# Loading the fifth granule's keys and queries ahead of the fourth granule's values

## The chip, the cores and the metric

The kernel runs on one core of a Trainium2 chip. The core has a matrix engine (TensorE, PE in the profile; its weight loads are PEld), a vector engine (VectorE, DVE), a scalar engine (ScalarE, ACT), GpSimd (POOL) and SyncE (SP), each with its own instruction stream in program order, and 16 DMA engines that serve several queues. The metric is the time of one execution on the device in microseconds (us); less is better. Four runs of the kernel before gave 208.94, 208.99, 209.06 and 209.45 us, median 209.03.

## The reference

Local attention with a few global keys, followed by a two-layer network. There are 4 batches, 8 heads, 768 positions and heads of 64 (q, k and v in float32).

```python
scores = (q @ k.T) / sqrt(64) - slope[h] * dist
keep   = (col < 8) | (0 <= row - col < 96)      # 8 global keys, a window of 96
a      = softmax(where(keep, scores, -1e9))
x      = (a @ v)                                # 4, 8, 768, 64 -> 3072 x 512
h      = relu(x @ w_in)                         # 512 x 2048
out    = (s * h * h + b) @ w_out                # 2048 x 512, float32
```

## The kernel before

The 3072 rows are cut into 12 granules of 256 positions (two blocks of 128), numbered j = 0 to 11, three per batch; granule j = 3 is the fourth, the first of batch 1, and j = 4 the fifth. A granule has 4 units, one per pair of heads, numbered u = 4j to 4j + 3. For a unit, `stage_S` multiplies keys and queries into a tile `ps_s`, ACT takes the exponential into `pt`, DVE multiplies a mask, and `stage_A` multiplies `pt` by the values into `ps_av` (L494) and normalizes the result into `xn`. `scores(s)` does `stage_S` for units 2s and 2s + 1. Scores need keys and queries with the head dimension on the partitions (`kx`, `qx`), while the loads bring them with the positions there (`nat`); so they are transposed: granules 0 to 3 by PE (`qk_first`, `qk_block`, `qk_wide`), granules from 4 on by four DMA transposes each on SP's queue (`qk_by_dma`, L359). Values are used as loaded, from `vbuf` (tile `vb`), one buffer per batch and two in turn. For a granule that isn't the first of its batch, `make_koff` (L382) and `make_voff` (L395) copy shifted keys and values; granule 4 thus also reads the values of granule 3.

The attention output is transposed (`xT`), and the network follows: `p1` (L618) is the first product with relu and square, `p2` (L666) the second; from granule 4 on the second product is done for pairs of granules by a scheme of seven half products (L818).

All loads of keys, queries, values and weights convert float32 to bfloat16 and stand in POOL's queue, in program order. A granule is six loads of 128 KB (as stored): `load_granule` (L110, its key and query loads at L116, the values through `load_v`, L104, at L108) issues keys and queries of block 0, keys and queries of block 1, then the two value loads. `load_qk` (L99) issues keys and queries of one block alone (L102). The weights and granules 0 to 3 are issued before any computation (L196 to L220), granules 4 and 5 from L1076 on, and granules 6 to 11 by `finish_granule` (L949), each after a gate that waits for earlier work. Nothing on POOL lies between the loads of granule 3 and those of granule 4, so the four granules 2 to 5 are one sequence of 24 loads on that engine.

The order on the other engines is written by hand (`manual_schedule`). Around the change: `qk_wide(3, ...)` at L1110 and L1113 transposes granule 3; SP takes `qk_by_dma(4)` (L1106), `load_scalars` (L1107) and `qk_by_dma(5)` (L1126) in this order; PE does `scores(6)` and `scores(7)` (granule 3), `stage_A(12)` to `stage_A(15)` (granule 3's values), `x_by_pe(3)`, and then `scores(8)` (L1135), the first that reads granule 4's transposes. `scores(10)`, in `step(9)`, is the first that reads granule 5's.

Of the kernel before, what the change touches and what calls it, by code (L numbers as in the profile page):

```python
# [17 lines left out]
def kernel(  # L18
# [21 lines left out]
    GB = 2  # L40
# [41 lines left out]
    def nat_tile(j):  # L82
        if j not in nat:
            nat[j] = ldp.tile([P, 2, GB, H, D], BF16, name="nat", tag=f"nat{j % 4}", bufs=1)
        return nat[j]
# [3 lines left out]
    def rows_of(src, b, sb):  # L89
        return src[b, :, sb * P : (sb + 1) * P, :].rearrange("h p d -> p h d")  # L90
# [8 lines left out]
    def load_qk(j, i):  # L99
        b, g = divmod(j, NGR)  # L100
        for n in range(2):
            nc.gpsimd.dma_start(nat_tile(j)[:, n, i, :, :], rows_of(srcs[n], b, g * GB + i))  # L102

    def load_v(j, blocks=range(GB)):  # L104
        b, g = divmod(j, NGR)
        for i in blocks:
            sb = g * GB + i
            nc.gpsimd.dma_start(vbuf[b % 2][:, sb, :, 0:D], rows_of(v, b, sb))  # L108

    def load_granule(j):  # L110
        b, g = divmod(j, NGR)
        t = nat_tile(j)
        for i in range(GB):
            sb = g * GB + i
            for n in range(2):
                nc.gpsimd.dma_start(t[:, n, i, :, :], rows_of(srcs[n], b, sb))  # L116
        load_v(j)
# [99 lines left out]
    for i in range(4):  # L217
        load_w_out(i, 4)
    load_granule(2)
    load_granule(3)  # L220

# [712 lines left out]
    def run(cs):  # L936
        for c in cs:
            c()
# [134 lines left out]
    run(sums[5:6])  # L1073
    p1[1][7]()
    run(sums[6:7])
    load_granule(4)  # L1076
    load_granule(5)
    template(range(H))
    lo = FC - FC // 4
# [167 lines left out]
```

The softmax here doesn't subtract the row's maximum and nothing guards it: scores larger than these inputs give would overflow.

## Time and profile before

| what | us |
|---|---|
| median of four runs | 209.03 |
| the profiled execution | 209.45 |
| its span, first to last instruction | 207.7 |
| PE busy | 202.0 |
| DVE busy | 160.3 |
| ACT busy | 128.7 |
| POOL busy | 69.9 |

The span is shorter than the time by 1.75 us, which lie ahead of the first and behind the last instruction. Lines of the profile name an instruction by engine, line of the kernel (L440), operation, and the tiles it writes and reads (`out<-in`); POOL's lines for loads are the time in which it writes out the transfer, not the transfer itself, whose time from issue to landing is asked for separately. SPq is SP's queue. `[0.64 <-DMA qx<-nat]` means that the engine was idle for 0.64 us and that a transfer ended the wait. In rows by stretches of time the columns are the length, the busy time of PE, PEld, DVE, ACT and POOL with the number of instructions, the granted clock, the share of the DMA engines and GB/s.

### The profile page before, as it was taken

The page shows a single profiled execution, that of the slowest core. Times are in us where ns is not written, and L with a number is a line of the kernel's source. Part 1 is how long each engine was busy: PE and PEld are TensorE (multiplying, and loading weights), DVE is VectorE, ACT ScalarE, POOL GpSimd, SP SyncE. Part 2 cuts the span into 40 slices and gives each one's busy share as a digit, 9 for nine tenths or more (in the row PEclk, how much of TensorE's full clock was granted, in tenths as well). Part 3 has the DMA queues.
Part 4 walks back from the last instruction along what each step waited for, and adds up shares of the span by engine and source line. Part 5 has one row for each costly group of instructions (what it writes and reads, how often), then busy time and mean ns, then how long its engine had stood idle before and what let it go on. Part 6 is the DMA issues. An engine that isn't in the chain of part 4 may idle for free.

```text
span 207.7 us, 5323 instructions
## 1 busy us (share of the span) xinstructions
PE 202.0 (97%) x2191; PEld 160.2 (77%) x2191; DVE 160.3 (77%) x336; ACT 128.7 (62%) x200; POOL 69.9 (34%) x90
## 2 busy tenths in 40 slices
PE   7899999999989999999999999999999999999993
PEld 2678884557866685778888898888898889888883
DVE  7686589977979955799799974699865696737974
ACT  4975669486975648786564495664695764476200
POOL 8986334899644300904700906300000000000000
PEclk9999999999999999999999999999999999999999
DMA  5999999999999999999999999995460300240006
GB/s 164 172 179 201 206 208 176 156 154 131 118 150 120 154 156 210 124 234 225 126 208 157 112 149 245 161 191 63 52 205 0 92 17 0 52 153 0 0 7 198
DMA packets 110836, 28.17 MB, mean 136 GB/s; under 512 B 97852, under 2 KB 109308, under 8 KB 110812
## 3 DMA queue, kind: packets, MB, share of 16 engines
q0 software_dynamic: 76000, 13.11, 88.2%
q1 hardware_dynamic: 33612, 14.13, 37.9%
q10 hardware_dynamic: 1200, 0.59, 1.1%
q8 instruction: 17, 0.28, 0.6%
q14 instruction: 7, 0.06, 0.1%
HBM read 27.26 MB, written 6.29 MB: 162 GB/s over the span
## 4 chain that ended last, share of the span: by engine, by line
PE 69%; DMA 20%; POOL 6%; SPq 2%; issue 1%; DVE 0%; POOLq 0%
PE ps L618 30%; PE ps L818 24%; DMA w_out_bf<-in_moe_w_out_dram 8%; PE ps L666 7%; DMA qx<-nat 4%; PE ps_s L440 4%; DMA vb<-in_v_dram 4%; PE ps_av L494 4%; DMA nat<-in_k_dram 3%; SPq L359 2%; POOL vb L108 2%; POOL nat L102 2%; POOL nat L116 1%; POOL w_in_bf L140 1%; PE ps_last L818 0%
## 5 line engine op out<-in xcount | busy, mean ns | idle before, releaser
L618 PE MATMUL ps<-xT,w_in_bf 128*128 128x256 bf16 x768 | 90.4, 273 | 0.0
L628 ACT ACTIVATE gT<-ps 128x512 bf16<-128x512 f32 x96 | 55.7, 598 | 46.8 <-PE ps L618 46.6
L618 PEld LDWEIGHTS <-w_in_bf 128*128 128x128 bf16 x768 | 73.0, 98 | 9.5 <-DVE xT L593 0.2
L449 ACT ACTIVATE pt<-ps_s 128x1024 bf16<-128x1024 f32 (+1 forms) x44 | 39.3, 945 | 3.4 <-PE ps_s L440 3.4
L666 PE MATMUL ps<-w_out_bf,gT 128*128 128x512 bf16 x128 | 29.7, 380 | 0.0
L456 DVE TENSOR_TENSOR pt<-pt,tmpl 128x1024 bf16<-128x1024 bf16 (+1 forms) x40 | 24.6, 646 | 4.5 <-ACT pt L449 4.3
L818 PEld LDWEIGHTS <-gsum 128*128 128x128 bf16 x256 | 24.2, 98 | 3.7 <-DVE gsum L781 0.5
L108 POOL DMA_DIRECT2D vb<-in_v_dram x24 | 21.4, 906 | 7.6 <-DMA w_out_bf<-in_moe_w_out_dram 3.3
L792 DVE TENSOR_TENSOR gT<-gT 128x1024 bf16<-128x1024 bf16 x20 | 13.7, 687 | 11.7 <-ACT gT L628 11.7
L666 PEld LDWEIGHTS <-gT 128*128 128x128 bf16 x128 | 11.8, 98 | 13.0
L465 DVE TENSOR_TENSOR xn<-ps_av,rc 128x256 bf16<-128x256 f32 x48 | 20.4, 425 | 1.7
L818 PEld LDWEIGHTS <-gT 128*128 128x128 bf16 x200 | 18.6, 98 | 2.3
L116 POOL DMA_DIRECT2D nat<-in_q_dram x20 | 18.0, 900 | 6.8 <-DMA nat<-in_q_dram 3.0
L116 POOL DMA_DIRECT2D nat<-in_k_dram x20 | 17.8, 890 | 6.4 <-DMA w_in_bf<-in_moe_w_in_dram 2.5
L464 DVE RECIPROCAL rc<-ps_av 128x4 f32<-128x4 f32 x48 | 8.6, 179 | 12.2 <-PE ps_av L494 10.3
L494 PEld LDWEIGHTS <-pt 128*128 128x128 bf16 x320 | 14.4, 97 | 2.7 <-DVE xn L465 0.7
L631 DVE TENSOR_TENSOR gT<-gT 128x512 bf16<-128x512 bf16 x32 | 13.0, 422 | 3.7 <-ACT gT L628 3.3
L494 PE MATMUL ps_av<-vb,pt 128*128 128x65 bf16 x208 | 15.4, 193 | 0.0
L818 PE MATMUL ps<-w_out_bf,gsum 128*128 128x256 bf16 x128 | 15.3, 273 | 0.0
L818 PE MATMUL ps<-wsub,gsum 128*128 128x256 bf16 x128 | 15.1, 273 | 0.0
L122 POOL COPY gate<-xT 1x1 bf16<-1x1 bf16 x6 | 1.9, 320 | 38.6 <-DMA xT<-xn 37.6
L818 PE MATMUL ps<-w_out_bf,gT 128*128 128x256 bf16 x120 | 13.9, 273 | 0.0
(111 smaller groups left out, 220.6 us busy)
## 6 DMA issues: line engine op xcount, KB each, us to landing
out_dram<-o_q SPq DMA_DIRECT2D x15, 256.0 KB, 2.4
vb<-in_v_dram POOLq DMA_DIRECT2D x24, 128.0 KB, 7.4
nat<-in_k_dram POOLq DMA_DIRECT2D x22, 128.0 KB, 6.5
nat<-in_q_dram POOLq DMA_DIRECT2D x22, 128.0 KB, 6.9
w_out_bf<-in_moe_w_out_dram POOLq DMA_DIRECT2D x4, 512.0 KB, 16.2
w_in_bf<-in_moe_w_in_dram POOLq DMA_DIRECT2D x4, 256.0 KB, 7.6
w_in_bf<-in_moe_w_in_dram POOLq DMA_DIRECT2D x2, 512.0 KB, 11.3
out_dram<-o_sb SPq DMA_DIRECT2D x4, 256.0 KB, 6.1
```

Source lines behind the costliest of these rows:

```text
L108: nc.gpsimd.dma_start(vbuf[b % 2][:, sb, :, 0:D], rows_of(v, b, sb))
L116: nc.gpsimd.dma_start(t[:, n, i, :, :], rows_of(srcs[n], b, sb))
L449: nc.scalar.activation(pt[:, :, 0:ncol], ps[:, :, 0:ncol], ACT.Exp, scale=QSCALE)
L456: nc.vector.tensor_tensor(pv, pv, m.rearrange("p h a c -> p h (a c)"), ALU.mult)
L465: nc.vector.tensor_tensor(dst, av[:, :, :, 0:D], rc[:].to_broadcast((P, 2, 2, D)), ALU.mult)
L494: nc.tensor.matmul(av[:, i, hi, 0 : D + 1], lhsT=pt[:, hi, c * P : (c + 1) * P], rhs=vv, start=(n == 0), stop=(n == len(terms) - 1),)
L618: nc.tensor.matmul(ps[:, i, :], lhsT=w_in_bf[:, kc, fc * P : (fc + 1) * P], rhs=xT[j][:, kc, :], start=(kc == 0), stop=(kc == KC - 1),)
L628: nc.scalar.activation(gs, ps[:], ACT.Relu)
L631: nc.vector.tensor_tensor(gs, gs, gs, ALU.mult)
L666: nc.tensor.matmul(po[:], lhsT=g_of(j)[:, fc, tb * P : (tb + 1) * P], rhs=w_out_bf[:, fc, :], start=(fc == 0), stop=(fc == FC - 1),)
L792: outs.append(lambda: nc.vector.tensor_tensor(gs, gs, gs, ALU.mult))
L818: nc.tensor.matmul(ps[:, tb, cs], lhsT=stat[:, fc, tb * P : (tb + 1) * P], rhs=mov[:, fc, cs], start=(fc == 0), stop=(fc == NH - 1),)
```

## The change

The two value loads of granule 3 are taken out of the opening loads and put behind the key and query loads of granule 4. The sequence on POOL was: k, q, k, q of granule 3, v, v of granule 3, k, q, k, q of granule 4, v, v of granule 4, granule 5. It becomes: k, q, k, q of granule 3, k, q, k, q of granule 4, v, v of granule 3, v, v of granule 4, granule 5.

```diff
@@ -217,7 +217,8 @@
     for i in range(4):
         load_w_out(i, 4)
     load_granule(2)
-    load_granule(3)
+    for i in range(GB):
+        load_qk(3, i)
@@ -1073,7 +1074,10 @@
     run(sums[5:6])
     p1[1][7]()
     run(sums[6:7])
-    load_granule(4)
+    for i in range(GB):
+        load_qk(4, i)
+    load_v(3)
+    load_v(4)
     load_granule(5)
     template(range(H))
```

## The prediction

> **What bounds the kernel now.** I read the page's totals first, then the chain, then the PE timeline at the place where the chain leaves PE, then POOL's and SP's timelines with the time each transfer took to land.
>
> ```profile
> PE 202.0 (97%) x2191; PEld 160.2 (77%) x2191; DVE 160.3 (77%) x336; ACT 128.7 (62%) x200; POOL 69.9 (34%) x90
> ...
> PE 69%; DMA 20%; POOL 6%; SPq 2%; issue 1%; DVE 0%; POOLq 0%
> ```
>
> PE is busy for 97% of the span at a granted clock of 0.999, so a change of load order can give back only gaps. Yet 20% of the chain is DMA. The chain's answer shows where:
>
> ```profile
> 40.28 6.70 DMA nat<-in_k_dram
> 46.99 0.02 issue
> 47.00 1.30 SPq L359
> ...
> 49.66 1.70 SPq L359
> ...
> 51.40 8.78 DMA qx<-nat
> 60.18 0.04 issue
> 60.22 0.57 PE ps_s L440 x14
> ```
>
> From 60.22 us to the end the chain is PE without a break worth counting. Before that it is: POOL's first key load of granule 4 (the fifth), issued at 40.28 and landed at 47.0; four transposes on SP (qk_by_dma(4)); the last one, issued at 51.40, lands at 60.18; scores(8) starts on it. That is the only place after the opening where a load stops PE. The PE timeline there, and the same group of instructions for the next scores, where nothing stopped it:
>
> ```profile
> 59.35 0.23 PE L440 MATMUL ps_s<-qx,kx 64*128 64x128 bf16 x2
> 60.22 0.34 PE L440 MATMUL ps_s<-qx,kx 64*128 64x128 bf16 x6 [0.64 <-DMA qx<-nat]
> 60.39 0.40 PE L440 MATMUL ps_s<-qx,ko 64*128 64x128 bf16 x8
> 60.72 0.39 PE L666 MATMUL ps<-w_out_bf,gT 128*128 128x512 bf16 x1
> ...
> 69.35 0.40 PE L440 MATMUL ps_s<-qx,kx 64*128 64x128 bf16 x8
> 69.58 0.39 PE L440 MATMUL ps_s<-qx,ko 64*128 64x128 bf16 x8
> 69.90 0.39 PE L666 MATMUL ps<-w_out_bf,gT 128*128 128x512 bf16 x1
> ```
>
> From the first score matmul to the next product it is 60.72 - 59.35 = 1.37 us with the wait and 69.90 - 69.35 = 0.55 us without. The stall costs 0.82 us, more than the 0.64 printed, because a modelled matmul end covers part of it. PE wants the transposed queries at about 59.4 and gets them at 60.18.
>
> **The change, part by part.** Nothing is added or taken away: the same loads, transposes and stores. Eight of POOL's loads change places, and only among themselves, since POOL has nothing else between granule 3's queries and granule 5. Their slots:
>
> ```profile
> 37.84 0.88 POOL L108 DMA_DIRECT2D vb<-in_v_dram  x1
> 39.17 0.87 POOL L108 DMA_DIRECT2D vb<-in_v_dram  x1 [0.45 <-DMA nat<-in_q_dram]
> 40.28 0.87 POOL L116 DMA_DIRECT2D nat<-in_k_dram  x1 [0.24 <-issue]
> 41.34 1.01 POOL L116 DMA_DIRECT2D nat<-in_q_dram  x1 [0.19 <-issue]
> 42.35 0.88 POOL L116 DMA_DIRECT2D nat<-in_k_dram  x1
> 43.21 0.90 POOL L116 DMA_DIRECT2D nat<-in_q_dram  x1
> ```
>
> The last two slots, for granule 4's values, follow at 44.08 and 44.97. Asking the trace slot by slot for the time to landing (7.3, 6.9, 6.7, 6.5, 6.4, 6.4, 6.4 and 6.2 us), the eight land at 45.1, 46.1, 47.0, 47.8, 48.75, 49.6, 50.5 and 51.2. All move 128 KB, all cost POOL 0.87 to 1.01 us, and POOL's waits here are on loads already under way, so a slot keeps its time whichever load stands in it. POOL's sum: 0.
>
> *Moved up:* granule 4's keys and queries take slots 1 to 4 instead of 3 to 6. The four landings go from 47.0, 47.8, 48.75, 49.6 to 45.1, 46.1, 47.0, 47.8: 1.7 to 1.9 us earlier.
>
> *Moved back:* granule 3's values take slots 5 and 6, landing at 48.75 and 49.6 instead of 45.1 and 46.1. Their first reader is stage_A(12), on PE at 53.16: 3.5 us to spare before contention. Granule 4's values stay in slots 7 and 8 (first reader make_voff(4), on DVE at 63.29), and granule 5's keys stay at 45.81.
>
> *What follows on SP:* its queue stands 45.2 us on the first key load, so qk_by_dma(4) starts 1.9 us earlier, at 45.1. Behind it are the two scalar loads and qk_by_dma(5). How much of the 1.9 us reaches the end of the transposes is the one term that the trace doesn't price directly. The transposes' packets (queue q1) first appear just before 50.0, 2.9 us after SP issued them, and then comes a bad patch:
>
> ```profile
> 48.00:50.00 2.00, 2.00 (x26) 1.31 (x24) 1.83 (x6) 1.37 (x2) 2.00 (x3) 1.00 2.68 151
> 50.00:52.00 2.00, 2.00 (x27) 1.64 (x27) 0.96 (x3) 2.00 (x5) 2.00 (x4) 1.00 1.82 106
> 52.00:54.00 2.00, 2.00 (x37) 1.78 (x34) 1.86 (x5) 2.00 (x5) 1.81 (x3) 1.00 4.20 55
> 54.00:56.00 2.00, 2.00 (x24) 1.75 (x19) 1.86 (x7) 1.99 (x4) 0.88 (x1) 1.00 2.01 162
> ```
>
> The last column is GB/s: 151, 106, 55, 162. A 16 KB transfer of the instruction queue starts at 50.5, and from 51 to 53.7 everything crawls; another starts at 62.2 and 62 to 64 shows the same (97 GB/s). I take that patch as fixed in time. Started at 48.0, q1 has about 450 packets more behind it when the patch begins than the 260 of before (252 in the window 50 to 51 now, about 400 per us later, in 58 to 59). At 400 per us those 450 are 1.1 us; the data of the second transpose would end some 1.4 us earlier. Upper end: all 1.9 us. Lower end: 0, if the patch begins with the transposes rather than with the instruction transfer. I take 1.2 us: the last transpose lands at 60.18 - 1.2 = 59.0, before PE's 59.4. The stall goes whole at any value from 0.8 up.
>
> *What the earlier transposes take from the loads.* With both queues running, 58 to 59 shows 430 load packets and 397 transpose packets, against 2374 load packets alone in 48 to 50, or 1187 per us. A load is 1024 such packets (128 KB at 128 bytes): 0.86 us alone, 2.4 us shared. Sharing would start at 48.0; the first load of granule 3's values is then nearly through, the second finishes about 1.6 us later than its slot, 51.2, which still leaves 2 us before 53.16. Bounds: 49.6 (no loss) and 53.9 (the whole 2.7 us patch falls on it as well), the latter 0.7 us too late. I take 0.
>
> The Trainium skill, "DMA: Bandwidth & Descriptors", section "Queues, rings and completion order", has each DMA engine alternate between the queues that have work, packet by packet. That speaks against the change: an earlier transpose takes half the packets of the values behind it. The 430 to 397 above agrees. By strict halves of 1187 per us the second value load would lose 0.9 us, by the row 1.6; neither reaches 53.16.
>
> *What is late next.* With PE 0.8 us ahead, scores(10) wants granule 5's last transpose at 69.41 - 0.82 = 68.6. It was issued at 59.45 and took 9.6 us: 69.05. If it does not move, PE stalls there for 0.46 us and 0.36 of the gain is left. It queues behind granule 4's transposes (issue at 59.45, 8 us under way), so I expect about 1 us of their lead to reach it: 0. Bounds 0 and +0.46. DVE and ACT are not in the way: make_koff(4) ends at 59.5, ACT's copy at 60.1, and the exponential follows the scores.
>
> *Sum* against the profiled execution: 209.45 (span 207.7 and 1.75 around it) - 0.82 = 208.63. That execution lies 0.42 above the median of the four, 209.03; on the median the sum is 208.21. If part of the 0.42 is a longer stall in the profiled execution, the others have less to win, down to 208.63 again. I take 208.35.
>
> **The rivals.**
> 1. *The stall shrinks or moves on* (18%): the transposes win only 0.3 to 0.7 us, or scores(10) waits up to 0.46. For it: slacks of 0.4 at both places. Against it: one chain of transposes feeds both. Gain 0.2 to 0.5 us: 208.5 to 208.8.
> 2. *Nothing moves* (10%): the crawl follows the transposes' start and sets their end. For it: GB/s falls 1 us after q1 starts. Against it: the same patch at 62 to 64 comes 1.5 to 2 us after the second set starts, with another instruction transfer. About 209.0.
> 3. *Slower: granule 3's values late at stage_A(12)* (16%). Place: PE at 53.16, with all later PE work behind it. It decides once the second value load lands after 53.16 plus the 0.82 us won, about 54.0; landing at 55 would cost 1.0 net, 210.0. For it: four slots back and into the start of the transposes; loads issued at 51 to 59 took 11.5 to 15.4 us to land. Against it: loads issued at 42.35 and 43.21 landed in 6.4.
> 4. Anything else that costs (4%), such as a crawl that now hits granule 5's loads as well: 209.5 to 210. A gain over 0.9 us: 2%.
>
> **How the numbers follow.** My forecast, the stall gone whole, has 50%: 208.1 to 208.65. What a measurement here can tell from no change is 0.2%, 0.42 us: faster is below 208.61, slower above 209.45. Faster: 47 of the forecast's 50, 9 of rival 1's 18, 2 for the larger gain: 58%. Same: 3 + 9 + 10 = 22%. Slower: 16 + 4 = 20%. The range must hold 80%: from 208.1 it takes the forecast, rivals 1 and 2 (78%) and the cheapest part of rival 3, to 209.4.
>
> **What would show it.** Right: POOL's keys and queries of granule 4 at 37.8 to 41.3, SP's first L359 near 45.1, the last transpose of granule 4 landed before 59.4, no wait of PE's L440 on qx, and 0.55 us between scores(8) and the next product. Wrong: a wait of PE's L494 on vb near 53 (rival 3), L440 waiting on qx near 60 (rivals 1 and 2) or near 68.6 (rival 1), or crawling windows that start 1 us after q1 does, wherever that is (rival 2).

## The result, and the profile after

| | median us | runs | span of the profiled execution |
|---|---|---|---|
| before | 209.34 | 56 | 207.7 |
| after | 208.68 | 35 | 206.7 |

The ratio is 0.9974, 95% interval 0.9964 to 0.9983: 0.54 us faster (0.36 to 0.75), out of 209.34; the two medians are 0.66 us apart. The 56 runs of before hold the four of the forecast, whose median of 209.03 was 0.3 us low. A second comparison (12 runs against 27, below) gave 0.9963 (0.9949 to 0.9977). Ratios leave out executions that ran longer at a lower granted clock, chiefly three of the six (at 0.983 and 0.984) of the version below that has granule 3's values late.

In the page of the changed kernel, the busy totals and the chain by engine:

```profile
PE 201.7 (98%) x2191; PEld 160.1 (77%) x2191; DVE 159.6 (77%) x336; ACT 128.6 (62%) x200; POOL 70.7 (34%) x90
...
PE 95%; DMA 2%; DVE 1%; ACT 0%; issue 0%
```

PE has the same 2191 matmuls and nearly the same busy time (201.7 against 202.0 us), in a span 1.0 us shorter. DMA's 20% of the chain has become 2%, all of it in the opening: from 5 us to the end nothing but PE (with a copy or two of DVE and ACT) is on it. PE's timeline at scores(8) and at scores(10) (the changed kernel has four lines more, so L440 is now L441 and L666 is L667):

```profile
59.27 0.40 PE L441 MATMUL ps_s<-qx,kx 64*128 64x128 bf16 x8
59.51 0.39 PE L441 MATMUL ps_s<-qx,ko 64*128 64x128 bf16 x8
59.83 1.90 PE L667 MATMUL ps<-w_out_bf,gT 128*128 128x512 bf16 x8
...
68.45 0.40 PE L441 MATMUL ps_s<-qx,kx 64*128 64x128 bf16 x8
```

From the first score matmul to the next product it is 59.83 - 59.27 = 0.56 us where it was 1.37, and the eight matmuls that stood as two and six are one group. PE starts scores(8) 0.08 us earlier than before and ends it 0.89 earlier; scores(10) is 0.90 earlier, and SP's last stores start 0.91 earlier (203.17 against 204.08). So 0.81 of the 0.91 us is the stall; 0.08 was there ahead of scores(8) and is put down to scatter of the opening. POOL's and SP's timelines show where the lead comes from:

```profile
38.13 0.87 POOL L102 DMA_DIRECT2D nat<-in_k_dram  x1
38.99 0.88 POOL L102 DMA_DIRECT2D nat<-in_q_dram  x1
39.86 1.09 POOL L102 DMA_DIRECT2D nat<-in_k_dram  x1
41.12 1.03 POOL L102 DMA_DIRECT2D nat<-in_q_dram  x1 [0.17 <-issue]
42.14 3.51 POOL L108 DMA_DIRECT2D vb<-in_v_dram  x4
```

```profile
45.00 1.31 SPq L360 DMA_TRANSPOSE kx<-nat  x1
46.36 1.31 SPq L360 DMA_TRANSPOSE qx<-nat  x1
47.71 1.37 SPq L360 DMA_TRANSPOSE kx<-nat  x1
49.12 1.76 SPq L360 DMA_TRANSPOSE qx<-nat  x1
...
59.81 1.22 SPq L360 DMA_TRANSPOSE qx<-nat  x1
```

And the fourth transpose, with the time from its issue to its landing:

```profile
L360 SPq DMA_TRANSPOSE qx<-nat x1: 1757/1757/1757, 49.1 to 49.1; - x1
DMA to landing us min/median/max: 9.2/9.2/9.2
```

SP's first transpose of granule 4 starts at 45.00 instead of 47.00. The last, issued at 49.12, took 9.2 us and landed at 58.3, against 60.18 before and against the 59.33 at which PE wants it. Granule 3's two value loads landed at 48.5 and 49.3, well before 53.1.

### The profile page after: what moved, and what is told of

Same layout as the page of the kernel before. It is cut to its first block, busy times and chain, and to the rows that moved or that the text cites. A ratio compares the mean times of both kernels' runs of the same rounds, so it can differ in the third digit from the quotient of the medians.

```text
span 206.7 us, 5323 instructions
## 1 busy us (share of the span) xinstructions
PE 201.7 (98%) x2191; PEld 160.1 (77%) x2191; DVE 159.6 (77%) x336; ACT 128.6 (62%) x200; POOL 70.7 (34%) x90
## 4 chain that ended last, share of the span: by engine, by line
PE 95%; DMA 2%; DVE 1%; ACT 0%; issue 0%
PE ps L619 41%; PE ps L819 24%; PE ps L667 14%; PE ps_s L441 6%; PE ps_av L495 5%; DMA first<-in_k_dram 2%; PE ps_t L351 1%; PE ps_s L517 1%; PE ps_x L591 1%; PE ps_s L532 1%; PE ps_av L558 1%; PE ps_t L327 1%; DVE nat L260 0%; PE ps_t L341 0%; PE ps_last L819 0%; DVE kx L331 0%
## 5 line engine op out<-in xcount | busy, mean ns | idle before, releaser
L667 PE MATMUL ps<-w_out_bf,gT 128*128 128x512 bf16 x128 | 29.7, 380 | 0.0
L793 DVE TENSOR_TENSOR gT<-gT 128x1024 bf16<-128x1024 bf16 x20 | 13.7, 687 | 11.7 <-ACT gT L629 11.7
L667 PEld LDWEIGHTS <-gT 128*128 128x128 bf16 x128 | 11.8, 98 | 13.0
L116 POOL DMA_DIRECT2D nat<-in_k_dram x16 | 14.2, 890 | 5.7 <-DMA w_in_bf<-in_moe_w_in_dram 2.4
L116 POOL DMA_DIRECT2D nat<-in_q_dram x16 | 14.3, 895 | 4.7 <-DMA nat<-in_q_dram 2.8
```

What stands on the lines that cost most here:

```text
L667: nc.tensor.matmul(po[:], lhsT=g_of(j)[:, fc, tb * P : (tb + 1) * P], rhs=w_out_bf[:, fc, :], start=(fc == 0), stop=(fc == FC - 1),)
L793: outs.append(lambda: nc.vector.tensor_tensor(gs, gs, gs, ALU.mult))
```

## Experiments

The theory: the change removes the stall at scores(8) by starting granule 4's transposes two load slots earlier, and does nothing else. The rivals: the two profiled executions differ by chance; the last load, not the transposes' queue, sets the end; the values moved back cost something; a second wait at scores(10) eats part of the gain; and the crawl of the transfers (a stretch of about a microsecond or more in which all DMA of the core falls far below its usual 150 GB/s or so), not the order of the loads, is what matters. Diffs are against the changed kernel unless it says otherwise.

**Both kernels again.** No edit.

> The kernel before, for a second profile of it. The first showed 0.82 us lost at scores(8). If the measured gain of 0.54 us is less than that because the stall varies from execution to execution, this profile shows another length of it, with the last transpose of granule 4 landing anywhere from 58.8 to 60.5. If the stall is the same 0.8 us in every execution, the changed kernel must lose some 0.3 us elsewhere.

> A third profile of the kernel before, to the same end: the three lengths of the stall at scores(8) should lie around 0.5 us in the mean if the stall is all that the change removes.

> The changed kernel once more. Theory: the gain is the stall at scores(8) and nothing else, so no wait of the scores line on qx near 59 us; the last transpose of granule 4 landed at 58.3 in the first trace of it, 1 us ahead of PE. The ratio to the kernel before should be 0.9974 again, within 0.002. The theory leaves one doubtful place: granule 5's last transpose landed 0.1 us before scores(10) wanted it (68.4 against 68.5), so this execution may show a wait of up to 0.5 us there. Rival, that the 1 us between the two profiled spans was mostly chance: the scores line waits near 59 again, and the ratio lies within 0.001 of 1.

> Another profile of the changed kernel: no wait on qx at scores(8); at scores(10) a wait between 0 and 0.5 us, by where granule 5's last transpose lands (68.4 in the first one).

PE's timeline at scores(8) in the two further profiles of the kernel before, the first and the second:

```profile
59.31 0.23 PE L440 MATMUL ps_s<-qx,kx 64*128 64x128 bf16 x2
60.66 0.34 PE L440 MATMUL ps_s<-qx,kx 64*128 64x128 bf16 x6 [1.11 <-DMA qx<-nat]
...
61.16 1.69 PE L666 MATMUL ps<-w_out_bf,gT 128*128 128x512 bf16 x6
```

```profile
59.56 0.23 PE L440 MATMUL ps_s<-qx,kx 64*128 64x128 bf16 x2
60.65 0.34 PE L440 MATMUL ps_s<-qx,kx 64*128 64x128 bf16 x6 [0.86 <-DMA qx<-nat]
...
61.15 1.69 PE L666 MATMUL ps<-w_out_bf,gT 128*128 128x512 bf16 x6
```

Measured as before (61.16 - 59.31 and 61.15 - 59.56, less 0.55), the stalls are 1.30 and 1.04 us. With the first profile's 0.82 there are three lengths, and the executions took 209.84, 209.83 and 209.45 us: all three are above the median, and the longer stalls go with the longer times. The last transpose landed at 60.64, 60.64 and 60.18. The mean of the three stalls is 1.05 us, not the 0.5 that was expected of it.

The changed kernel's two further profiles have no wait on qx at either place; the last transpose of granule 4 landed at 58.9 and 58.2, and the one of granule 5 0.8 and 1.3 us ahead of scores(10), against 0.1 in the first. Timed again, the ratio to before was 0.9963 (0.9949 to 0.9977), with the runs of before between 208.55 and 209.94 and those of after between 208.39 and 208.83. So the stall is real and varies from execution to execution; three profiles of the changed kernel show none, and its times scatter less. In the first comparison the changed kernel scatters more than here: 10 of its 35 times lie between 209.02 and 209.96; none of these has been profiled, and what delays them is open. That the gain by the ratios (0.54 and 0.77 us) is below the mean of the three profiled stalls fits executions of before with little or no stall, and the fastest one of before, 208.45 us, is as fast as the fastest of after, 208.44; but none of those has been profiled, so this part is argued, not shown.

**Half of the change.**

```diff
-    for i in range(GB):
-        load_qk(4, i)
+    load_qk(4, 0)
     load_v(3)
+    load_qk(4, 1)
     load_v(4)
```

> Half of the change: only block 0 of granule 4's keys and queries goes ahead of granule 3's values; block 1 keeps its two slots (landing about 48.8 and 49.6). Theory A, the transposes' own queue sets the end: once the first of the four starts 1.9 us early, the third has its input (48.8) long before the queue reaches it (about 54), and the last lands near 58.3, as with the whole change: no stall at scores(8), ratio to before 0.9965 to 0.9985. Theory B, the last load sets the end: the fourth transpose is issued at about 50.1 instead of 51.4 and lands 0.6 us or less earlier than before, near 59.6; some 0.2 us of the stall is left, ratio 0.998 to 1.0.

Ratio 0.9965 (0.9952 to 0.9979): all of the gain. SP's timeline of this run:

```profile
45.09 1.29 SPq L360 DMA_TRANSPOSE kx<-nat  x1
46.42 1.31 SPq L360 DMA_TRANSPOSE qx<-nat  x1
48.66 1.73 SPq L360 DMA_TRANSPOSE kx<-nat  x1
50.43 1.26 SPq L360 DMA_TRANSPOSE qx<-nat  x1
```

and for the last of the four:

```profile
DMA to landing us min/median/max: 8.0/8.0/8.0
```

The last transpose is issued 1.3 us later than with the whole change and takes 8.0 us instead of 9.2: it lands at 58.43, no later than the 58.2 to 58.9 there. So theory A holds. The four transposes behave as if they ran one after the other in their queue: as long as the crawls are the same (more on these below), the start of the first decides when the last ends, and the loads of block 1 need not move.

**The values of granule 3 two slots later, and later still.** In the first, the two value loads change places:

```diff
+    load_v(4)
     load_v(3)
-    load_v(4)
     load_granule(5)
```

> The changed kernel with the two pairs of value loads exchanged: granule 4's first, then granule 3's, two slots later than in the change. Those slots landed at 49.8 and 51.6 in the changed kernel's trace, 1.5 us before stage_A(12) wants granule 3's values (53.1). Theory, a value load costs nothing until it lands after 53.1: no wait of L495 on vb, ratio to before 0.9955 to 0.9975, as the changed kernel. Rival, the spare time is eaten in part of the executions by the crawl near 50: a wait of up to 1 us on vb, and a ratio above 0.998.

Ratio 0.9966 (0.9951 to 0.9982), no wait on vb; the two loads landed at 49.8 and 51.6. In the second, they stand behind granule 5's first keys and queries as well:

```diff
-    load_v(3)
     load_v(4)
-    load_granule(5)
+    load_qk(5, 0)
+    load_v(3)
+    load_qk(5, 1)
+    load_v(5)
```

> The prediction's rival 3 made on purpose. Order: keys and queries of granule 4, values of granule 4, keys and queries of block 0 of granule 5, and only then the two value loads of granule 3, then the rest of granule 5. Granule 3's values stand in the slots that landed at 53.1 and 56.2 in the changed kernel, where stage_A(12) wants them at 53.1. If a late value load holds up PE one to one, PE's L495 waits on vb for 2.5 to 3.5 us near 53 and the kernel is 1.5 to 3 us slower than before (ratio 1.007 to 1.015), scores(8) having no stall. If the wait at stage_A(12) is absorbed (PE's work behind it was waiting for something else anyway), the ratio stays under 1.002.

Ratio 1.0128 (1.0083 to 1.0173), 2.7 us slower than before, from three executions only (211.02, 211.57 and 213.40 us). The second value load landed at 56.2, and PE's timeline has:

```profile
53.44 0.22 PE L495 MATMUL ps_av<-vb,pt 128*128 128x65 bf16 x2
56.23 0.46 PE L495 MATMUL ps_av<-vb,pt 128*128 128x65 bf16 x10 [2.56 <-DMA vb<-in_v_dram]
56.62 0.51 PE L441 MATMUL ps_s<-qx,kx 64*128 64x128 bf16 x12
```

where the changed kernel has:

```profile
53.08 0.53 PE L495 MATMUL ps_av<-vb,pt 128*128 128x65 bf16 x12
53.55 0.51 PE L441 MATMUL ps_s<-qx,kx 64*128 64x128 bf16 x12
```

The wait is passed on one to one: from its first matmul to the next scores, stage_A(12) takes 56.62 - 53.44 = 3.18 us instead of 53.55 - 53.08 = 0.47, which is 2.7 us more, and the span is 209.8 us, 2.8 more than in the changed kernel of the same comparison (207.0). So rival 3 of the forecast is a real mechanism. A landing at 51.6 cost nothing and one at 56.2 cost its whole lateness, which fits the 53.1 us at which PE wants the values; the change, at 49.3, stays 3.8 us on the safe side.

**Granule 5 ahead as well.**

```diff
     load_v(3)
+    for i in range(GB):
+        load_qk(5, i)
     load_v(4)
-    load_granule(5)
+    load_v(5)
```

> One step more than the change: granule 5's four key and query loads also go ahead of granule 4's values (order: keys and queries of 4, values of 3, keys and queries of 5, values of 4, values of 5). Theory: in the changed kernel granule 5's last transpose lands only 0.1 us before scores(10) wants it, and in a good part of the executions later, which is why the measured gain (0.54 us) is less than the 0.9 us of the profiled one. Two slots earlier, its loads land 1.7 us or more earlier, the last transpose lands before 67.5, and the time goes 0.1 to 0.4 us below the changed kernel's (ratio to before 0.9955 to 0.997). Rival: the second wait is not there in most executions (the stall of before is just shorter on the average than in its profile); then the ratio equals the changed kernel's, 0.9974 within 0.0005. Price of the step: granule 4's values, wanted at 63 by DVE, land two to four slots later, by about 59: nothing.

Ratio 0.9964 (0.9952 to 0.9976), the same as the changed kernel beside it (0.9963). Granule 5's last transpose landed at 65.95 instead of 68.4, and nothing came of it. The rival holds: no second wait eats the gain.

**The instruction transfers moved, with the load order of before.** Against the kernel before, one kernel with 36 and one with 18 opening matmuls:

```diff
-    warm(9, 4 * P)
+    warm(36, P)
```

```diff
-    warm(9, 4 * P)
+    warm(18, 2 * P)
```

The columns worked through are the same; PE has 54 or 18 more instructions (a weight load and a matmul for each of 27 or 9).

> The kernel before, with the 9 opening matmuls of 512 columns (on zeros, for warming) made 36 of 128 columns: the same columns, but 54 more instructions on PE, so that the 16 KB transfers of the instruction queue, one for every 256 instructions or so, come some 2.5 us earlier: the one at 50.5 at about 48, before granule 4's transposes move (49.9). Theory F, the crawl of 51 to 53.7 comes from the instruction transfer that meets the transposes: it is gone or much shorter, the last transpose lands at 58 to 59 and the stall at scores(8) goes, without any change of the load order; 0.3 to 0.9 us less, if the opening keeps its length. Theory T, the crawl comes 1 us after the transposes start, whatever the instruction queue does: it stays near 51 to 53, and so do the stall and the time. The changed kernel's trace had one crawl of each kind (49 to 50 with no instruction transfer, 54 to 55 after one at 52.9).

> The kernel before with the opening matmuls made 18 of 256 columns: 18 more instructions on PE, a third of the shift of the 36. The instruction transfer should start near 49.3 instead of 50.5, still beside the first transposes (49.9). Theory, the length of the crawl depends on whether a 16 KB transfer runs while transposes run: the crawl stays 2 to 2.75 us long and the stall stays above 0.4 us; ratio to before 0.999 to 1.001. Rival, any earlier transfer helps in proportion: the stall is cut by about a third, ratio 0.999 to 0.9995 with a last transpose at about 59.9; or the 36 helped by their shape rather than by the shift: no stall here either.

Ratios: 0.9982 (0.9967 to 0.9997) with 36 matmuls, 0.9968 (0.9953 to 0.9983) with 18. Neither profile has a wait of PE on qx, the load order being that of before. With 18, the last transpose landed at 59.05; with 36 at 59.23, just as PE came to it (from the first score matmul to the next product 59.79 - 59.13 = 0.66 us, 0.1 more than without a wait), so that some of the other executions may well have kept a short stall. Rows by 1 us of the kernel before and of the one with 18 matmuls; the last column is GB/s:

```profile
50.00:51.00 1.00, 1.00 (x18) 0.74 (x18) 0.41 (x2) 1.00 (x3) 1.00 (x2) 1.00 2.83 161
51.00:52.00 1.00, 1.00 (x12) 0.90 (x10) 0.54 (x1) 1.00 (x3) 1.00 (x3) 1.00 0.82 51
52.00:53.00 1.00, 1.00 (x12) 0.90 (x10) 0.86 (x3) 1.00 (x4) 1.00 (x3) 1.00 7.65 61
53.00:54.00 1.00, 1.00 (x27) 0.88 (x25) 1.00 (x3) 1.00 (x3) 0.81 (x1) 1.00 0.76 49
```

```profile
50.00:51.00 1.00, 1.00 (x18) 0.72 (x15) 0.28 (x1) 1.00 (x3) 1.00 (x2) 1.00 2.37 151
51.00:52.00 1.00, 1.00 (x12) 0.90 (x10) 0.56 (x1) 1.00 (x3) 1.00 (x3) 1.00 1.67 62
52.00:53.00 1.00, 1.00 (x11) 0.90 (x10) 0.97 (x2) 1.00 (x3) 1.00 (x3) 1.00 2.21 152
53.00:54.00 1.00, 1.00 (x27) 0.83 (x26) 0.94 (x3) 0.99 (x3) 0.90 (x2) 1.00 1.80 148
```

Both start their transposes just before 50 and crawl from 51 to 52. Only the kernel before goes on crawling to 54. Its 16 KB instruction transfer starts at 50.5, after the transposes have begun; with 18 matmuls it starts at 48.9, with 36 at 46.9, and the crawl is over after 1 us. A finer view of the kernel before, GB/s in 40 slices of 52 to 53 us, shows that its crawl is really two, with a recovery between:

```profile
GB/s 184 97 174 154 128 149 154 154 149 109 144 149 138 118 72 31 31 31 15 20 21 31 20 10 20 20 10 10 10 10 10 10 5 10 10 10 10 5 10 0
```

So neither theory holds alone. There is a crawl of about 1 us, falling to some 40 GB/s, that follows the transposes' start by about 1 us whatever the instruction queue does (theory T; it is there in all 13 profiles). And there is a second one, near 10 GB/s, from 52.4 to 53.7 in the kernel before, where an instruction transfer starts while transposes run (theory F). The expectation for 18 matmuls was wrong: a transfer at 48.9 is early enough.

The changed kernel has both crawls as well, each 1 to 2 us behind its cause; its transposes start at 48.0 and its instruction transfer at 52.9:

```profile
49.00:50.00 1.00, 1.00 (x15) 0.66 (x15) 0.97 (x3) 0.93 (x2) 1.00 (x3) 1.00 1.68 79
50.00:51.00 1.00, 1.00 (x17) 0.73 (x16) 0.33 (x1) 1.00 (x3) 1.00 (x4) 1.00 2.10 157
...
53.00:54.00 1.00, 1.00 (x28) 0.83 (x26) 0.99 (x3) 1.00 (x3) 0.66 (x1) 1.00 2.06 140
54.00:55.00 1.00, 1.00 (x12) 0.90 (x11) 0.91 (x4) 0.99 (x3) 0.21 (x1) 1.00 2.20 45
55.00:56.00 1.00, 1.00 (x12) 0.90 (x10) 0.96 (x5) 1.00 (x3) 0.00 (x0) 1.00 1.28 101
```

**Both together.** The changed kernel with `warm(36, P)`:

> The changed kernel with the 36 short opening matmuls, which bring the instruction transfers forward (to 46.9 and 60.4 in the kernel before). In the kernel before, that shift alone took the stall at scores(8) away and 0.18% of the time. Theory: the shift helps only through the stall; the changed kernel has none left, so nothing more is won: ratio to before 0.9955 to 0.9975. Rival: the short matmuls win something of their own in the opening; then the ratio falls by about 0.002, to 0.994 to 0.9955.

Ratio 0.9966 (0.9954 to 0.9978), the last transpose of granule 4 landing at 57.6, 0.6 us or more earlier than in any other run, for nothing. The shift helps only through the stall; there is one stall to remove, and either of the two edits removes it, the shift by 54 instructions all but 0.1 us in its one profile. No version beat the changed kernel.

All 13 profiles together show how the two edits add up. From the start of the first transpose on SP to the landing of the last it is 12.9 to 13.7 us in the ten in which an instruction transfer falls among the transposes, whatever the load order, and 12.1 to 12.4 us in the three in which it comes earlier. So the load order moves the start by 1.9 us, and an instruction transfer among the transposes goes with about 1 us more.

## Why the prediction was right, point by point

*The stall at scores(8) is the only loss to win back: right, as far as these edits reach.* With the last transpose landing anywhere from 57.6 to 59.05 and the values in time, the ratios are 0.9963 to 0.9974, however it was brought about, and every profile without a wait of PE on a transfer has a span of 206.7 to 207.0 us.

*POOL's slots keep their times whichever load stands in them: right.* The first five of the eight stood at 37.84, 39.17, 40.28, 41.34 and 42.35 before and stand at 38.13, 38.99, 39.86, 41.12 and 42.14 now, within 0.4 us; the landings are within 0.3 us of the forecast's for six slots and within 0.7 for all eight.

*How much of the 1.9 us of lead reaches the end of the transposes, taken as 1.2: mis-sized.* It was 1.9 in the first pair of profiles; the means of three against three are 60.49 and 58.46, 2.0 us. The step that failed is "I take that patch as fixed in time". The patch is two crawls, one tied to the transposes' start, so that it moves with them, and one tied to an instruction transfer, which itself started at 52.9 instead of 50.5. The lower end had its reason the wrong way round: a patch that begins with the transposes moves with them and lets the whole 1.9 us through, not 0. The 450 packets don't follow from the rows named either: 1.9 us at about 400 packets per us are some 760. As the stall was gone at any value from 0.8 up, these errors cost the forecast nothing.

*What the earlier transposes take from the value loads, landing taken as 51.2: too late by 1.9 us.* The second one landed at 49.3, its slot's time. The ratio of 430 load packets to 397 transpose packets came from 58 to 59 us, well into the transposes; in the first microsecond of sharing, 48 to 49, the changed kernel moved 842 load packets (q0) and 181 of transposes (q1):

```profile
q0 software_dynamic: 842, 0.11, 208.6%
q1 hardware_dynamic: 181, 0.05, 46.9%
```

The equal halves that the forecast took from the Trainium skill's rule ("DMA: Bandwidth & Descriptors", "Queues, rings and completion order") are not seen there either.

*Rival 2, that the crawl follows the transposes' start: true of 1 us of it, but "nothing moves" does not follow.* That part did move with them, from the microsecond 51 to 52 to that of 49 to 50, and so did the end of the transposes, about 8 us behind it in either order (60.2 and 58.3).

*What is late next, scores(10): no stall, as taken.* Granule 5's last transpose landed at 67.9 in the mean of three profiles after, against 69.0 before, which is the lead of about 1 us that the forecast expected. The margin was thin in one profile (0.1 us) and comfortable in two.

*The sum.* The profiled execution gave back 0.81 us of the 0.82, but the ratio only 0.54. The forecast had named why: the profiled execution could hold a longer stall than the others. The term that was mis-sized is the stall of a median execution. The base was off as well: the four runs' median of 209.03 is 209.34 with 56. From its own base the forecast's 208.35 is a gain of 0.68 us, which the interval of 0.36 to 0.75 still holds. That it comes so near is in part luck, since 0.68 was chosen between 0.40 and 0.82 and not worked out. The measured median of 208.68 lies just above the 208.1 to 208.65 of the forecast's own case and among rival 1's times; what tells the two apart is that no profile of the changed kernel has a wait at either place.

## What to carry to other kernels

Where a queue of loads feeds a chain of transfers that must run one after the other, order the loads by when the first link of the chain can start, not by granule: the first link's start set the last link's end here, and what was put back (values wanted 7 us or more after they had landed) had spare time that could be read from landing and first use. A wait of PE on a transfer is priced by comparing the same group of instructions with and without it (1.37 against 0.55 us), since the printed idle time was 0.64. And one profile shows one execution: three profiles of this kernel gave stalls of 0.82, 1.04 and 1.30 us, so a forecast on the median should not take one as it stands.

## What the runs showed of the hardware

Eighteen more instructions on PE, far from the place in time and without visible effect on PE's own work, were worth about as much as the change of the load order (0.9968 against 0.9963 and 0.9974). The instruction queue's transfer before and with 18 more instructions, in the DMA view of the microsecond 50 to 51 and 48 to 49:

```profile
q8 instruction: 1, 0.02, 14.9%
```

```profile
q8 instruction: 1, 0.02, 8.8%
```

The page counts 17 of them and 0.28 MB. More instructions on PE alone moved them earlier (36.5 and 50.5 us became 34.2 and 48.9 with 18, 33.0 and 46.9 with 54), so they are taken to be PE's instruction fetch. The Trainium skill, "Runtime: NRT & Kernel Launch", "Instruction fetch mechanics", has the instructions refilled in 16 KB blocks of 256 by the engine's own DMA queue, which fits the 17 here (2191 matmuls and as many weight loads are 17 times 256), and calls the cost mostly hidden. No wait of PE on one shows in these profiles; but a transfer that started while transposes were in flight was followed, 0.9 to 2.2 us later, by 0.4 to 1.4 us in which all DMA fell from about 150 to some 10 GB/s. Between 50 and 66 us the 13 profiles have 23 such transfers, and it is so at every one. The transfers at 33.0 to 48.9 us, ahead of the first DMA transposes, were followed by no such fall. Why the transfer starts at 52.9 to 53.2 in the changed order and at 50.3 to 50.9 in the old one, PE's instructions being the same and the transfers ahead of it (36.4 to 36.8) and behind it (62.0 to 62.9, the version with late values apart) standing at the same times, is not explained; nor is the 1 us crawl at the start of granule 4's transposes.
